# Decode attention: values two tiles behind their scores

## The chip, the cores and the metric

The kernel runs on one core of one Trainium2 chip. The metric is the time of one execution on the device, in microseconds (us), as the median of several runs. In the rows, PE is TensorE (PEld its weight loads), DVE is VectorE, ACT is ScalarE, POOL is GpSimd, and SP is the engine whose queue issues the loads.

## What is computed

One decode step of attention: 8 batches of 32 heads, one query row for each, 4096 keys and values of 128 elements, all in bf16.

```python
B, H, Sq, Skv, Dh = 8, 32, 1, 4096, 128

def reference(q, k, v):
    scale = q.shape[-1] ** -0.5
    scores = jnp.einsum('bhqd,bhkd->bhqk', q, k) * scale
    attn = _softmax(scores, axis=-1)
    return jnp.einsum('bhqk,bhkd->bhqd', attn, v)
```

Every head has its own K and V, and each element of them is used once: 256 heads x 4096 x 128 x 2 bytes = 268 MB for K and the same for V, 536.9 MB in all.

## The kernel before, in words

The 256 heads are taken four at a time: a tile is 4 heads, so there are 64 tiles (NT). A tile's K is one buffer of 128 partitions x 128 positions x 128 elements (4 MB); 32 partitions hold one head. V has the same form. K and V tiles share one pool of five buffers (SLOTS, tag `kv`), filled by `load` (line 98) from the SP queue: one DMA for a tile, but four pieces for the last V.

The work of a tile t is cut into functions, whose instructions the rows name by line and by tile:

- `product(t, lo, hi)` (line 126): VectorE multiplies K by the query row in place (line 132) and adds the two halves of each row of 128 (line 135), 32 positions at a time, so four such pairs make a tile. It is called for the first half and for the second half of the positions.
- `sum_over_d(t)` (line 142): TensorE sums the 64 remaining elements of each position down to 4, with 16 matmuls against the identity into `ps` (line 149). Each of the 16 reads all positions, so all need the whole product.
- `weights_of(t)` (line 156): VectorE reduces `ps` to the scores `sc` (line 159), takes their maximum (`pmax`, `spread`, `nmax`, lines 163 to 170) and makes `bias` (line 174); ScalarE does four exponentials, one for each head, into the weights `w` with their sums in `esum` (line 180); TensorE adds the sums over the partitions (`zp`, line 185) and VectorE takes the reciprocal `rz` (line 187).
- `values_of(t)` (line 192): TensorE multiplies weights and V in 32 matmuls into `av` (line 197), ScalarE copies the result to `comb` (line 202), four small matmuls put its diagonal blocks together in `op` (line 205), and ScalarE scales it by `rz` into `stage` (line 212). The results of eight tiles leave together (line 216).

The query rows are spread over the partitions by `q_prep` (line 112), once for four tiles.

The loop over t (lines 220 to 232) loads K of t+1 and V of t, and then does the first half of t's product, the weights of t-1, the second half of t's product, the values of t-1, and the sums of t. The program's order is a priority: the tile framework puts each engine's instructions in order by it and by when it takes them to be ready, hands out the buffers of a pool as they come free, and sets the semaphores. Each engine, and each queue of loads, then runs its own list strictly in order. So in the rows the weights of a tile (`sc` to `bias`) are woven into the second half of the next tile's product, and four of the 16 sums of t stand ahead of the values of t-1 on TensorE, the other twelve behind them.

A load needs a free buffer. K's buffer is free when the 16 sums of its tile are done, V's when the 32 matmuls of `av` are.

Of the kernel before, what the change touches and what calls it, by code (L numbers as in the profile page):

```python
# [19 lines left out]
def kernel(  # L20
# [15 lines left out]
    NT = NH // G  # L36
# [14 lines left out]
    kv_pool = ctx.enter_context(tc.tile_pool(name="kv_pool", bufs=SLOTS))  # L51
    consts = ctx.enter_context(tc.tile_pool(name="consts", bufs=1))
    q_pool = ctx.enter_context(tc.tile_pool(name="q_pool", bufs=2))
    w_pool = ctx.enter_context(tc.tile_pool(name="w_pool", bufs=2))
    small = ctx.enter_context(tc.tile_pool(name="small", bufs=3))
    o_pool = ctx.enter_context(tc.tile_pool(name="o_pool", bufs=2))
    ps_s = ctx.enter_context(tc.tile_pool(name="ps_s", bufs=2, space=bass.MemoryType.PSUM))
    ps_v = ctx.enter_context(tc.tile_pool(name="ps_v", bufs=2, space=bass.MemoryType.PSUM))
# [39 lines left out]
    def load(kind, t):  # L98
        src = k_t if kind == "k" else v_t
        buf = kv_pool.tile([P, C, D], BF16, name=f"{kind}t", tag="kv")  # L100
        cuts = [C]
        if kind == "v" and t == NT - 1:
            cuts = [C // 2, C // 4, C // 8, C // 8]
        c0 = 0
        for n in cuts:
            nc.sync.dma_start(buf[:, c0 : c0 + n, :], src[t, :, c0 : c0 + n, :])
            c0 += n
        loads[kind, t] = buf
# [3 lines left out]
    def q_prep(t):  # L112
        if t % QN == 0:
            qrow = q_pool.tile([G, QN, D], BF16, name="qrow", tag="qrow")
            nc.gpsimd.dma_start(qrow[:], q_g[:, t : t + QN, :])  # L115
            qp = ps_q.tile([P, QN * D], F32, name="qp", tag="qp")
            nc.tensor.matmul(  # L117
                qp[:], lhsT=sel[:], rhs=qrow.rearrange("g n d -> g (n d)"), start=True, stop=True
            )
            qb = q_pool.tile([P, QN, D], BF16, name="qb", tag="qb")  # L120
            nc.scalar.activation(out=qb.rearrange("p n d -> p (n d)"), in_=qp[:], func=ACT.Copy)  # L121
            qbs[t // QN] = qb

    state = {}

    def product(t, lo, hi):
        kt = loads["k", t]
        qb = qbs[t // QN]
        j = t % QN
        for c0 in range(lo, hi, MC):  # L130
            part = kt[:, c0 : c0 + MC, :]
            nc.vector.tensor_tensor(  # L132
                out=part, in0=part, in1=qb[:, j : j + 1, :].to_broadcast([P, MC, D]), op=ALU.mult
            )
            nc.vector.tensor_tensor(  # L135
                out=part[:, :, 0 : D // 2], in0=part[:, :, 0 : D // 2],
                in1=part[:, :, D // 2 : D], op=ALU.add,
            )
# [3 lines left out]
    def sum_over_d(t):  # L142
        kt = loads.pop(("k", t))
        sums[t] = []
        for u in range(NU):
            ps = ps_s.tile([P, UC, DS], F32, name="ps", tag="ps")
            n = D // 2 // DS
            for s in range(n):
                nc.tensor.matmul(  # L149
                    ps[:], lhsT=ident[:],  # L150
                    rhs=kt[:, u * UC : (u + 1) * UC, s * DS : (s + 1) * DS],
                    start=(s == 0), stop=(s == n - 1),
                )
            sums[t].append(ps)

    def weights_of(t):
        sc = small.tile([P, C], F32, name="sc", tag="sc")
        for u, ps in enumerate(sums.pop(t)):
            nc.vector.tensor_reduce(  # L159
                out=sc[:, u * UC : (u + 1) * UC], in_=ps[:], axis=AX.X, op=ALU.add  # L160
            )
        pmax = small.tile([P, 1], F32, name="pmax", tag="pmax")
        nc.vector.tensor_reduce(out=pmax[:], in_=sc[:], axis=AX.X, op=ALU.max)  # L163
        spread = small.tile([P, 32], F32, name="spread", tag="spread")
        nc.vector.tensor_scalar(  # L165
            out=spread[:], in0=zero[:], scalar1=pmax[:, 0:1], scalar2=-scale,
            op0=ALU.add, op1=ALU.mult,
        )
        nmax = small.tile([P, 1], F32, name="nmax", tag="nmax")
        nc.vector.tensor_reduce(  # L170
            out=nmax[:], in_=spread[:], axis=AX.X, op=ALU.min, apply_transpose=True
        )
        bias = small.tile([P, G], F32, name="bias", tag="bias")
        nc.vector.tensor_scalar(  # L174
            out=bias[:], in0=own[:], scalar1=nmax[:, 0:1], scalar2=None, op0=ALU.add
        )
        w = w_pool.tile([P, C, G], BF16, name="w", tag="w")
        esum = small.tile([P, G], F32, name="esum", tag="esum")
        for g in range(G):
            nc.scalar.activation(  # L180
                out=w[:, :, g], in_=sc[:], func=ACT.Exp, bias=bias[:, g : g + 1], scale=scale,
                accum_out=esum[:, g : g + 1],
            )
        zp = ps_z.tile([G, 1], F32, name="zp", tag="zp")
        nc.tensor.matmul(zp[:], lhsT=esum[:], rhs=ones[:], start=True, stop=True)  # L185
        rz = small.tile([G, 1], F32, name="rz", tag="rz")
        nc.vector.reciprocal(out=rz[:], in_=zp[:])  # L187
        state[t] = (w, rz)

    stages = {}  # L190

    def values_of(t):
        w, rz = state.pop(t)
        vt = loads.pop(("v", t))
        av = ps_v.tile([CB * G, CB * D], F32, name="av", tag="av")
        for c0 in range(0, C, CB):
            nc.tensor.matmul(  # L197
                av[:], lhsT=w[:, c0 : c0 + CB, :], rhs=vt[:, c0 : c0 + CB, :],
                start=(c0 == 0), stop=(c0 == C - CB),
            )  # L200
        comb = small.tile([CB * G, CB * D], BF16, name="comb", tag="comb")
        nc.scalar.activation(out=comb[:], in_=av[:], func=ACT.Copy)  # L202
        op = ps_o.tile([G, D], F32, name="op", tag="op")
        for m in range(CB):
            nc.tensor.matmul(  # L205
                op[:], lhsT=ident[0 : CB * G, m * G : (m + 1) * G],
                rhs=comb[:, m * D : (m + 1) * D], start=(m == 0), stop=(m == CB - 1),
            )
        if t % ON == 0:
            stages[t // ON] = o_pool.tile([G, ON, D], BF16, name="stage", tag="stage")  # L210
        stage = stages[t // ON]
        nc.scalar.activation(out=stage[:, t % ON, :], in_=op[:], func=ACT.Copy, scale=rz[:, 0:1])  # L212
        if t == NT - 1 or t == NT - 2 or (t % ON == ON - 1):
            lo = {NT - 1: NT - 1, NT - 2: NT - ON}.get(t, t - ON + 1)
            eng = nc.scalar if t == NT - 1 else nc.gpsimd
            eng.dma_start(o_g[:, lo : t + 1, :], stage[:, lo % ON : t % ON + 1, :])

    q_prep(0)
    load("k", 0)
    for t in range(NT):  # L220
        if t + 1 < NT:
            load("k", t + 1)
        load("v", t)
        if t + 2 < NT:
            q_prep(t + 2)
        product(t, 0, C // 2)
        if t > 0:
            weights_of(t - 1)
        product(t, C // 2, C)
        if t > 0:  # L230
            values_of(t - 1)
        sum_over_d(t)
    weights_of(NT - 1)
    values_of(NT - 1)


# [28 lines left out]
```

## Time and profile before

| what | value |
|---|---|
| median of 3 runs | 1394.6 us (1394.41 to 1395.68) |
| the profiled execution | 1393.52 us, of which the span from the first to the last instruction is 1391.7 us |
| bytes read | 536.94 MB, 386 GB/s over the span |
| mean granted TensorE clock | 0.807 of the full clock |

The profile is of one execution. Its rows give starts in us from the beginning of the span. In a timeline, "x4" is a run of four such instructions on one engine, with the start of the first and the time to the end of the last; in brackets stands the idle time of the engine ahead of it and who ended it. In the windows, the granted clock is a share of the full one: 1.00 is 2.4 GHz, and 0.50 is 1.2 GHz. The DMA share is the busy share of the core's 16 DMA engines; it can come out a little over 1.

### The profile page before, as it was taken

To read this page: it belongs to the slowest core of one execution; us is meant where nothing else is said; L and a number is where in the kernel's file an instruction comes from. 1 tells how busy PE (TensorE), PEld (TensorE's weight loads), DVE (VectorE), ACT (ScalarE), POOL (GpSimd) and SP (SyncE) were. 2 spreads that over 40 slices of the span, in tenths; PEclk is the share of its full clock that TensorE was granted. 3 is DMA by queue.
4 is the path that set the end of the run, shared out by engine and by line. 5 is a ranking of instruction groups with operands and counts; after the bars stand their busy time and mean duration, and the time that the engine had idled before them with its cause. 6 is when DMAs were issued, how large, how long until landed. Compare 5 with 4: busy or idle time off the path is not lost.

```text
span 1391.7 us, 9050 instructions
## 1 busy us (share of the span) xinstructions
PE 856.0 (62%) x3472; PEld 305.0 (22%) x3472; DVE 946.5 (68%) x898; ACT 182.3 (13%) x657; POOL 15.7 (1%) x36
## 2 busy tenths in 40 slices
PE   2557557566576575675665755756657557566566
PEld 0212122122122221221222212212212222122122
DVE  6766766767667667676776677676766766767662
ACT  0111111111111111111111111111111111111111
POOL 1000000000000000000000000000000000000000
PEclk9887878788787887877878878788787878788788
DMA  9999999999999899999999999999999999989970
GB/s 407 427 431 433 425 388 398 409 378 408 379 391 420 368 404 393 392 392 392 398 401 388 382 407 393 382 401 386 412 392 377 411 378 390 421 364 407 393 332 1
DMA packets 19683, 537.59 MB, mean 386 GB/s; under 512 B 2776, under 2 KB 2844, under 8 KB 3128
## 3 DMA queue, kind: packets, MB, share of 16 engines
q1 hardware_dynamic: 18864, 536.88, 92.1%
q8 instruction: 27, 0.44, 0.1%
q0 software_dynamic: 768, 0.14, 0.1%
q14 instruction: 16, 0.13, 0.0%
q10 hardware_dynamic: 8, 0.00, 0.0%
HBM read 536.94 MB, written 0.07 MB: 386 GB/s over the span
## 4 chain that ended last, share of the span: by engine, by line
PE 52%; DVE 38%; ACT 8%; issue 1%; DMA 1%; DVEq 0%; ACTq 0%
PE av L197 37%; DVE kt L132 21%; PE ps L149 13%; DVE kt L135 11%; ACT w L180 8%; DVE sc L159 3%; PE op L205 1%; DVE pmax L163 1%; DMA kt<-in_k_dram 1%; PE zp L185 1%; DVE bias L174 1%; DVE spread L165 1%; DVE nmax L170 1%; DVEq L159 0%; ACTq L180 0%
## 5 line engine op out<-in xcount | busy, mean ns | idle before, releaser
L132 DVE TENSOR_TENSOR kt<-kt,qb 128x4096 bf16<-128x4096 bf16 x256 | 577.6, 2275 | 12.4 <-DMA kt<-in_k_dram 12.4
L149 PE MATMUL ps<-kt,ident 128*128 128x512 bf16 x1024 | 308.3, 440 | 410.8 <-DVE kt L135 410.2
L197 PE MATMUL av<-vt,w 128*16 128x512 bf16 x2048 | 523.6, 420 | 0.0
L135 DVE TENSOR_TENSOR kt<-kt 128x2048 bf16<-128x2048 bf16 x256 | 305.1, 1210 | 0.0
L197 PEld LDWEIGHTS <-w 128*16 128x16 bf16 x2048 | 193.8, 97 | 299.1 <-issue 102.8
L149 PEld LDWEIGHTS <-ident 128*128 128x128 bf16 x1024 | 95.2, 103 | 666.9 <-issue 591.7
L159 DVE TENSOR_REDUCE sc<-ps 128x128 f32<-128x512 f32 x64 | 44.2, 691 | 283.8 <-PE ps L149 283.8
L180 ACT ACTIVATE w<-sc,bias 128x128 bf16<-128x128 f32 x256 | 110.8, 567 | 505.9 <-DVE bias L174 505.9
L202 ACT ACTIVATE comb<-av 16x512 bf16<-16x512 f32 x64 | 37.6, 587 | 532.9 <-PE av L197 532.9
L187 DVE RECIPROCAL rz<-zp 4x1 f32<-4x1 f32 x64 | 9.9, 155 | 135.4 <-PE zp L185 135.4
L117 PE MATMUL qp<-qrow,sel 4*128 4x512 bf16 x16 | 9.3, 582 | 110.4 <-ACT qb L121 95.6
L180 ACT ACTIVATION_READ_ACCUMULATOR w<-sc,bias 128x1 f32 x256 | 64.6, 252 | 0.0
L212 ACT ACTIVATE stage<-op,rz 4x128 bf16<-4x128 f32 x64 | 22.9, 358 | 44.2 <-PE op L205 44.2
L121 ACT ACTIVATE qb<-qp 128x512 bf16<-128x512 f32 x16 | 9.6, 597 | 122.9 <-DVE kt L132 114.0
L205 PE MATMUL op<-comb,ident 16*4 16x128 bf16 x256 | 24.3, 213 | 0.7 <-ACT comb L202 0.7
L185 PEld LDWEIGHTS zp<-ones,esum 128*4 128x4 f32 x128 | 5.8, 84 | 68.3 <-ACT w L180 68.3
L185 PE MATMUL zp<-ones,esum 128*4 128x1 f32 x128 | 12.3, 165 | 10.7 <-ACT w L180 4.2
L205 PEld LDWEIGHTS <-ident 16*4 16x4 bf16 x256 | 12.4, 78 | 27.8 <-issue 27.8
L115 POOL DMA_DIRECT2D qrow<-in_q_dram x16 | 9.3, 581 | 756.5 <-PE qp L117 756.5
L163 DVE TENSOR_REDUCE pmax<-sc 128x1 f32<-128x128 f32 x64 | 17.8, 278 | 0.0
L165 DVE TENSOR_SCALAR spread<-zero,pmax 128x32 f32<-128x32 f32 x64 | 15.0, 234 | 0.0
L174 DVE TENSOR_SCALAR bias<-own,nmax 128x4 f32<-128x4 f32 x64 | 14.3, 223 | 0.0
(18 smaller groups left out, 22.8 us busy)
## 6 DMA issues: line engine op xcount, KB each, us to landing
kt<-in_k_dram SPq DMA_DIRECT2D x64, 4096.0 KB, 19.9
vt<-in_v_dram SPq DMA_DIRECT2D x63, 4096.0 KB, 12.8
vt<-in_v_dram SPq DMA_DIRECT2D x1, 2048.0 KB, 14.3
vt<-in_v_dram SPq DMA_DIRECT2D x1, 1024.0 KB, 16.4
vt<-in_v_dram SPq DMA_DIRECT2D x2, 512.0 KB, 17.6
qrow<-in_q_dram POOLq DMA_DIRECT2D x16, 4.0 KB, 6.8
out_dram<-stage POOLq DMA_DIRECT2D x7, 8.0 KB, 6.7
out_dram<-stage POOLq DMA_DIRECT2D x1, 7.0 KB, 1.9
```

Of the source, the lines that this page charges most:

```text
L132: nc.vector.tensor_tensor(out=part, in0=part, in1=qb[:, j : j + 1, :].to_broadcast([P, MC, D]), op=ALU.mult)
L135: nc.vector.tensor_tensor(out=part[:, :, 0 : D // 2], in0=part[:, :, 0 : D // 2], in1=part[:, :, D // 2 : D], op=ALU.add,)
L149: nc.tensor.matmul(ps[:], lhsT=ident[:], rhs=kt[:, u * UC : (u + 1) * UC, s * DS : (s + 1) * DS], start=(s == 0), stop=(s == n - 1),)
L159: nc.vector.tensor_reduce(out=sc[:, u * UC : (u + 1) * UC], in_=ps[:], axis=AX.X, op=ALU.add)
L163: nc.vector.tensor_reduce(out=pmax[:], in_=sc[:], axis=AX.X, op=ALU.max)
L165: nc.vector.tensor_scalar(out=spread[:], in0=zero[:], scalar1=pmax[:, 0:1], scalar2=-scale, op0=ALU.add, op1=ALU.mult,)
L174: nc.vector.tensor_scalar(out=bias[:], in0=own[:], scalar1=nmax[:, 0:1], scalar2=None, op0=ALU.add)
L180: nc.scalar.activation(out=w[:, :, g], in_=sc[:], func=ACT.Exp, bias=bias[:, g : g + 1], scale=scale, accum_out=esum[:, g : g + 1],)
L185: nc.tensor.matmul(zp[:], lhsT=esum[:], rhs=ones[:], start=True, stop=True)
L197: nc.tensor.matmul(av[:], lhsT=w[:, c0 : c0 + CB, :], rhs=vt[:, c0 : c0 + CB, :], start=(c0 == 0), stop=(c0 == C - CB),)
L202: nc.scalar.activation(out=comb[:], in_=av[:], func=ACT.Copy)
L205: nc.tensor.matmul(op[:], lhsT=ident[0 : CB * G, m * G : (m + 1) * G], rhs=comb[:, m * D : (m + 1) * D], start=(m == 0), stop=(m == CB - 1),)
```

## The change

The values of a tile are taken two tiles after its scores. The loop does the values of t-2 where it did those of t-1, and the last two tiles' values stand behind the loop. The sum of the weights and its reciprocal (`zp`, `rz`) move from `weights_of` to the head of `values_of`. V's loads move back by one place: K0 and K1 are loaded ahead of the loop, and turn t loads K of t+2 and then V of t. The weights get three buffers for two, and the small tiles four for three. The five buffers of K and V stay.

```diff
-    w_pool = ctx.enter_context(tc.tile_pool(name="w_pool", bufs=2))
-    small = ctx.enter_context(tc.tile_pool(name="small", bufs=3))
+    w_pool = ctx.enter_context(tc.tile_pool(name="w_pool", bufs=3))
+    small = ctx.enter_context(tc.tile_pool(name="small", bufs=4))
...
                 accum_out=esum[:, g : g + 1],
             )
+        state[t] = (w, esum)
+
+    stages = {}
+
+    def values_of(t):
+        w, esum = state.pop(t)
         zp = ps_z.tile([G, 1], F32, name="zp", tag="zp")
         nc.tensor.matmul(zp[:], lhsT=esum[:], rhs=ones[:], start=True, stop=True)
         rz = small.tile([G, 1], F32, name="rz", tag="rz")
         nc.vector.reciprocal(out=rz[:], in_=zp[:])
-        state[t] = (w, rz)
-
-    stages = {}
-
-    def values_of(t):
-        w, rz = state.pop(t)
         vt = loads.pop(("v", t))
...
     load("k", 0)
+    load("k", 1)
     for t in range(NT):
-        if t + 1 < NT:
-            load("k", t + 1)
+        if t + 2 < NT:
+            load("k", t + 2)
         load("v", t)
...
         product(t, C // 2, C)
-        if t > 0:
-            values_of(t - 1)
+        if t > 1:
+            values_of(t - 2)
         sum_over_d(t)
     weights_of(NT - 1)
+    values_of(NT - 2)
     values_of(NT - 1)
```

## Rows read from the trace of the kernel before

**Rows 1.** The page: busy time of the engines, and transfers in 40 slices

```profile
PE 856.0 (62%) x3472; PEld 305.0 (22%) x3472; DVE 946.5 (68%) x898; ACT 182.3 (13%) x657; POOL 15.7 (1%) x36
...
DMA  9999999999999899999999999999999999989970
GB/s 407 427 431 433 425 388 398 409 378 408 379 391 420 368 404 393 392 392 392 398 401 388 382 407 393 382 401 386 412 392 377 411 378 390 421 364 407 393 332 1
```

**Rows 2.** Waits of the engines: who waited for whom, us in total, times, longest

```profile
DVE sc L159 <- PE ps L149: 283.8, 63, 10.5
DVE rz L187 <- PE zp L185: 135.4, 64, 2.4
...
DVE kt L132 <- DMA kt<-in_k_dram: 12.4, 1, 12.4
```

**Rows 3.** Waits of the load queue (SP), same columns

```profile
SPq L106 <- PE av L197: 1085.3, 61, 18.8
```

**Rows 4.** Timeline of one tile: start us, us, engine, line, operation, [idle before]

```profile
607.08 0.69 DVE L159 TENSOR_REDUCE sc<-ps 128x128 f32<-128x512 f32 x1 [3.82 <-PE ps L149]
...
614.82 0.22 DVE L174 TENSOR_SCALAR bias<-own,nmax 128x4 f32<-128x4 f32 x1
614.96 1.87 PE L149 MATMUL ps<-kt,ident 128*128 128x512 bf16 x4 [7.98 <-DVE kt L135]
...
616.98 9.16 PE L197 MATMUL av<-vt,w 128*16 128x512 bf16 x32
...
617.24 4.46 DVE L132 TENSOR_TENSOR kt<-kt,qb 128x4096 bf16<-128x4096 bf16 x2
617.36 0.13 PEld L197 LDWEIGHTS <-w 128*16 128x16 bf16 x1 [0.29 <-issue]
...
620.77 0.13 PEld L197 LDWEIGHTS <-w 128*16 128x16 bf16 x1 [0.29 <-issue]
...
621.63 2.34 DVE L135 TENSOR_TENSOR kt<-kt 128x2048 bf16<-128x2048 bf16 x2
...
626.08 1.04 PE L149 MATMUL ps<-kt,ident 128*128 128x512 bf16 x4
...
629.37 0.69 DVE L159 TENSOR_REDUCE sc<-ps 128x128 f32<-128x512 f32 x1 [5.39 <-PE ps L149]
```

**Rows 5.** Timeline, load queue (SP): the first V that waited, and the last

```profile
50.90 0.33 SPq L106 DMA_DIRECT2D vt<-in_v_dram  x1
...
1330.25 4.96 SPq L106 DMA_DIRECT2D vt<-in_v_dram  x5
```

**Rows 6.** Windows: us, busy of PE, PEld, DVE, ACT, POOL, granted clock, DMA share, GB/s

```profile
52.00:100.00 48.00, 27.67 (x120) 10.05 (x118) 34.41 (x34) 6.31 (x22) 0.57 (x1) 0.85 1.00 431
100.00:148.00 48.00, 28.76 (x112) 10.10 (x111) 32.72 (x32) 6.51 (x26) 0.00 (x0) 0.75 1.00 431
...
400.00:800.00 400.00, 254.50 (x1031) 90.49 (x1031) 275.60 (x261) 53.87 (x195) 4.04 (x7) 0.80 0.94 393
```

**Rows 7.** Windows over one `av`, same columns

```profile
616.98:621.20 4.22, 4.22 (x12) 1.28 (x13) 4.04 (x3) 0.00 (x0) 0.00 (x0) 0.50 0.88 380
621.20:626.07 4.87, 4.87 (x23) 1.92 (x21) 2.77 (x3) 0.00 (x0) 0.00 (x0) 0.99 0.75 320
```

**Rows 8.** Timeline, the first product

```profile
13.39 4.49 DVE L132 TENSOR_TENSOR kt<-kt,qb 128x4096 bf16<-128x4096 bf16 x2 [12.41 <-DMA kt<-in_k_dram]
```

**Rows 9.** Timeline of the tail

```profile
1364.27 7.59 PE L197 MATMUL av<-vt,w 128*16 128x512 bf16 x32
...
1375.08 0.69 DVE L159 TENSOR_REDUCE sc<-ps 128x128 f32<-128x512 f32 x1 [10.48 <-PE ps L149]
...
1376.65 0.23 DVE L174 TENSOR_SCALAR bias<-own,nmax 128x4 f32<-128x4 f32 x1
...
1378.81 8.75 PE L197 MATMUL av<-vt,w 128*16 128x512 bf16 x32
...
1387.60 0.59 ACT L202 ACTIVATE comb<-av 16x512 bf16<-16x512 f32 x1 [8.90 <-PE av L197]
```

## The prediction

> **What bounds the kernel now.** I read the page first, to see which resource has no slack in any slice. It shows no simple answer [rows 1]: TensorE is busy for 62% of the span, VectorE for 68%, the transfers look nearly full in every slice, and yet the rate falls from 427 to 433 GB/s in slices 2 to 4 to about 390 later. So I asked the waits who is late. VectorE waited for a K tile once in the whole run, at the very start, for 12.4 us [rows 2]; no compute instruction waits for V at all. It waited 283.8 us for the sums of the products (`ps`), and 135.4 us for the sum of the weights (`zp`). The load queue, on the other side, stood 1085.3 us waiting for the values' matmuls (`av`) to give a buffer back [rows 3]. The data are early, the buffers are late: a loop of compute sets the pace, and the transfers follow it.
>
> The loop is read from one tile in the timeline [rows 4]. From `sc` at 607.08 to the end of `bias` at 615.04 VectorE needs 7.96 us (it does the second half of the next tile's product in between). Then ScalarE's four exponentials, until `av` starts at 616.98: 1.94 us. Then the 32 matmuls of `av`, until the sums go on at 626.08: 9.10 us. Then the remaining 12 sums and the four `op` matmuls, until the next `sc` at 629.37: 3.29 us. Together 22.29 us, and every link waits for the one before. This tile is one of the long ones: from V_2's issue at 50.90 to V_62's at 1330.25 [rows 5] it is 1279.35 / 60 = 21.32 us a tile.
>
> What the transfers could do is seen where they had not yet been held up: 431 GB/s at a share of 1.00 between 52 and 148 us, against 393 at 0.94 later [rows 6]. Each load is 4.194 MB, so one takes 4.194 / 0.431 = 9.73 us and a tile (K and V) 19.46 us. That is 1.86 us under the loop.
>
> **The change, part by part.** *The lag.* `av` of tile t-2 takes weights that were finished a tile ago. So it leaves the loop: after the sums of t-1, TensorE can run `av` of t-2 while VectorE works on tile t, and the sums of t follow the product of t. VectorE's own work for a tile is 7.96 us for `sc` to `bias` with the second half, and 623.97 - 617.24 = 6.73 us for the first half [rows 4]: 14.7 us. TensorE's, at the full clock: 12 sums and 4 `op` in 3.2 us and 4 sums at about 0.24, so some 3.8 us for 16 sums; and `av` in 9.1 us as it is here, which holds a stretch at half the clock (0.50 from 616.98 to 621.20, then 0.99) [rows 7]. That makes 13.4 us with `op`. Both are under 19.46, and they overlap but for sums and `sc`. So the loop gives way and the transfers bind.
>
> *Do the buffers then let the transfers run without a gap?* Loads go out as K0, K1, K2, V0, K3 at once; each further one needs a release. Releases come as sums 0, sums 1, values 0, sums 2, values 1, ..., so V1 follows sums 0, K4 sums 1, V2 values 0, K5 sums 2: V_t follows values t-2, and K_(t+3) follows sums t. Let K_t land at X. VectorE ends its product at X + 14.7; V_(t-2) lands at X + 9.7; values t-2 run to about X + 18.8, sums t to X + 23. V_t is issued at X + 18.8 and the stream comes to it at X + 38.9; K_(t+3) at X + 23, and the stream comes to it at X + 48.6. Each has 20 us in hand. VectorE needs sums t for `sc` only after the first half of t+1, at X + 26.2. So every wait of a tile is hidden under the stream; where this cover is thinnest (3 us, before `sc`), losing it delays VectorE, which has 19.46 - 14.7 = 4.8 us of slack a tile.
>
> *K ahead of V.* The queue issues the same 131 loads. V_0 lands one place (9.7 us) later; its use moves a whole tile later. Cost nil.
>
> *`zp` and the reciprocal.* Same instructions, 0.15 us on VectorE. The 2.1 us wait of each [rows 2] was for exponentials that are now a tile old: it goes, off the path that binds, so I count nothing; were `zp` queued behind a late `av`, the wait would come out of the 4.8 us. *The extra buffers* (3 and 4) only keep the longer-lived tiles; nothing.
>
> *The end.* The first K landed at 13.39 [rows 8]. The last load is number 127 after it: 13.39 + 127 x 9.73 = 1249.1; V_61 is 1229.6, V_62 1239.4. From there: values 61 to 1238.1 (8.5 us, half of it at the lower clock), sums 63 to 1241.9, `sc` to `av` takes 3.7 us in today's tail, so the last weights are ready by 1245.6 beside values 62 (7.6 us in the tail [rows 9], to 1249.5), and values 63 to 1257.1. From the end of the last `av` to the end of the span 4.1 us pass today (1387.6 to 1391.7, with `comb`, `op`, stage and store): 1261.2. The added values of tile 62 cost 7.6 us of this, as they now stand behind the last sums. The profiled execution took 1393.5 us for a span of 1391.7, and the median of the runs is 1.1 us above it: 1261.2 + 1.8 + 1.1 = **1264 us**, 9.4% below 1394.6. A gain of 130 us is 62 tiles by 1.86 = 115, and the rest from the tail: today 61 us of compute follow the issue of the last V [rows 5].
>
> **The rivals.** *1. The stream does not hold 431.* The later windows move 393 at 0.94, which is 418 at a full share [rows 6]; I take the gaps for late issues, but they could be the price of busier engines on the same memory, and VectorE is to be busier still. At 418 a load takes 10.03 us, the last lands at 1287, and the time is 1302. Chance 0.13. At its harshest the stream could give no more than the run's mean of 386 [rows 1]: 536.9 / 0.386 = 1391 us for the loads, no gain; 96 us at 431 speak against it: 0.01. The Trainium skill (DMA: Bandwidth & Descriptors, Bandwidth) says that loads from HBM are bound by some 358 GB/s for a core; an estimate from that page's figure is 1500 us for these loads alone. The trace speaks against it: this very kernel averaged 386 GB/s. The same section gives 425 GB/s measured for a lone 16 MB load, an estimate of 1263 us for the loads and so some 1278 in all, between my two cases.
>
> *2. `sc` in front of the first half (slower than before).* The order of each engine is the scheduler's, and a scheduler that believes the K tile late may put `sc` to `bias` of t ahead of the whole product of t+1. Then VectorE stands still during the sums, and the loop is product (2 x 6.73 = 13.5), 16 sums, and `sc` to `bias` alone (1375.08 to 1376.88 in the tail, 1.8 [rows 9]). With sums at 3.8 us this is 19.1, still under the stream; with TensorE at the lower clock, where a matmul takes 0.426 us (its weight loads go from 617.36 to 620.77 in 8 steps [rows 4], at 0.50 [rows 7]), the sums take 6.8 and the loop 22.1 us: 62 x 0.78 = 48 us more, **1443 us**. It decides from sums of 6.0 us on (21.32 - 15.3). For it: TensorE would idle before the sums, and idle stretches are followed by half the clock today. Against: today's order has the first half in front all through. Chance 0.06.
>
> *3. TensorE at the lower clock throughout.* 48 matmuls at 0.426 and 0.6 us of others are 21.0 us a tile: 62 x 1.54 = 95 more than forecast, 1359. It needs the clock never to rise in a stretch of 13 us; today it does after 4 to 6. Chance 0.05.
>
> *4. The edit does not move `av`.* TensorE's queue today runs 4 sums before `av` [rows 4]. If it keeps that order, those 4 take the time of the exponentials and the loop stays: 7.96 + 1.9 + 9.1 + 3.3, no change, 1395. They came first, though, since the weights were not there, which now they are. Chance 0.03.
>
> **How the numbers follow.** Forecast 0.72, rival 1 0.13 (and 0.01 without a gain), 2 0.06, 3 0.05, 4 0.03. Faster by over 0.2% (2.8 us, about what a measurement of this kernel can tell from no change): 0.72 + 0.13 + 0.05 = 0.90; within it 0.04; slower 0.06. The range takes forecast and rival 1: down to 1252 (433 GB/s as in the best slice takes 5 us off, an `av` of the last tile that runs beside its pieces' landing another 7), up to 1312 (rival 1 and 10 us for a tail at the lower clock). It leaves out 0.15.
>
> **What would show it.** Right: VectorE's largest wait becomes a K transfer, some 4 us a tile; TensorE waits for V at `av`; GB/s is near 431 in all slices but the last; the load queue still waits, but each load is issued some 20 us before its first packet; `av` starts before the product of the same turn ends. Wrong: 415 to 420 GB/s at a full share (1); `sc` directly behind `ps` with VectorE idle in between (2); a granted clock near 0.5 (3); `av` still behind 4 sums (4).

## The result and the profile after

The changed kernel takes 1269.5 us (median of 4 runs, 1268.67 to 1270.69) against 1394.6 us (4 runs): a ratio of 0.910, 95% interval 0.909 to 0.912. Forecast were 1264 us in a range of 1252 to 1312. The profiled execution took 1270.69 us for a span of 1268.9 us.

The page of the changed kernel: busy times, transfers in 40 slices, and the shares of the chain that ended last.

```profile
PE 847.7 (67%) x3472; PEld 315.7 (25%) x3472; DVE 939.4 (74%) x898; ACT 181.7 (14%) x657; POOL 15.8 (1%) x36
...
DMA  9999999999999999999999999999999999999994
GB/s 397 433 431 432 432 431 429 431 432 429 430 430 429 431 433 431 430 430 431 430 430 433 430 431 431 429 431 430 433 429 430 433 430 433 430 429 430 430 432 178
...
DMA 69%; PE 25%; DVE 5%; ACT 0%; issue 0%; ACTq 0%; DVEq 0%
```

No engine became quicker: the busy times are those of before to within 11 us [rows 1]. What changed is the row of GB/s. It stands at 429 to 433 in every slice between the first and the last, where before it fell to about 390 [rows 1, 6], and the chain that sets the end runs through transfers for 69% of the span.

The waits of the changed kernel (who waited for whom: us in total, times, longest):

```profile
PE av L197 <- DMA vt<-in_v_dram: 349.0, 57, 7.9
DVE kt L132 <- DMA kt<-in_k_dram: 283.5, 57, 12.3
...
DVE sc L159 <- PE ps L149: 28.2, 5, 11.5
```

Against [rows 2] the direction has turned round. VectorE's wait for the sums fell from 283.8 to 28.2 us, and its wait for a K tile rose from 12.4 us (once) to 283.5 us (57 times, 5 us each). TensorE waits for V, which nobody did before. The load queue still waits:

```profile
SPq L106 <- PE av L197: 572.2, 61, 21.4
```

These 572.2 us are put down to `av` (1085.3 before [rows 3]), and another 560 us to V's transfers and to `zp`. But its waits now cost nothing: the median time from issue to landing is 29.8 us for a V and 35.5 us for a K (12.8 and 19.9 before), which less one transfer of 9.7 us leaves some 20 and 26 us in hand.

One tile in the timeline of the changed kernel (start, us, engine, line, operation, [idle before]), to be laid beside [rows 4]:

```profile
600.51 4.50 DVE L132 TENSOR_TENSOR kt<-kt,qb 128x4096 bf16<-128x4096 bf16 x2 [4.72 <-DMA kt<-in_k_dram]
...
607.20 0.68 DVE L159 TENSOR_REDUCE sc<-ps 128x128 f32<-128x512 f32 x1
...
610.25 8.99 PE L197 MATMUL av<-vt,w 128*16 128x512 bf16 x32 [6.85 <-DMA vt<-in_v_dram]
...
614.97 0.21 DVE L174 TENSOR_SCALAR bias<-own,nmax 128x4 f32<-128x4 f32 x1
...
619.17 1.04 PE L149 MATMUL ps<-kt,ident 128*128 128x512 bf16 x4
...
619.93 4.49 DVE L132 TENSOR_TENSOR kt<-kt,qb 128x4096 bf16<-128x4096 bf16 x2 [4.76 <-DMA kt<-in_k_dram]
```

The row to read first is `av`: it starts at 610.25, ahead of `bias` at 614.97, so its weights are a turn old; before, it stood 2 us behind `bias` [rows 4]. A tile takes 619.93 - 600.51 = 19.42 us, twice a load, and both engines stand idle for a transfer once in it (4.7 and 6.9 us).

### The profile page after: what moved, and what is told of

The parts are those of the page before. It is cut to its first block, busy times and chain, and to the rows that moved or that the text cites. A ratio compares the mean times of both kernels' runs of the same rounds, so it can differ in the third digit from the quotient of the medians.

```text
span 1268.9 us, 9053 instructions
## 1 busy us (share of the span) xinstructions
PE 847.7 (67%) x3472; PEld 315.7 (25%) x3472; DVE 939.4 (74%) x898; ACT 181.7 (14%) x657; POOL 15.8 (1%) x36
## 4 chain that ended last, share of the span: by engine, by line
DMA 69%; PE 25%; DVE 5%; ACT 0%; issue 0%; ACTq 0%; DVEq 0%
DMA vt<-in_v_dram 68%; PE av L197 24%; DVE kt L132 3%; DVE kt L135 1%; PE ps L149 1%; DMA kt<-in_k_dram 1%; ACT w L180 0%; DVE sc L159 0%; PE op L205 0%; ACT comb L202 0%; DVE pmax L163 0%; DVE spread L165 0%; DVE bias L174 0%; ACT qb L121 0%; PE qp L117 0%
## 5 line engine op out<-in xcount | busy, mean ns | idle before, releaser
L197 PE MATMUL av<-vt,w 128*16 128x512 bf16 x2048 | 573.8, 450 | 349.0 <-DMA vt<-in_v_dram 349.0
L132 DVE TENSOR_TENSOR kt<-kt,qb 128x4096 bf16<-128x4096 bf16 x256 | 579.4, 2285 | 283.5 <-DMA kt<-in_k_dram 283.5
L197 PEld LDWEIGHTS <-w 128*16 128x16 bf16 x2048 | 208.8, 102 | 696.4 <-issue 529.8
L149 PE MATMUL ps<-kt,ident 128*128 128x512 bf16 x1024 | 248.7, 385 | 24.0 <-DVE kt L135 24.0
L149 PEld LDWEIGHTS <-ident 128*128 128x128 bf16 x1024 | 89.6, 97 | 156.4 <-issue 58.9
L159 DVE TENSOR_REDUCE sc<-ps 128x128 f32<-128x512 f32 x64 | 43.8, 684 | 28.2 <-PE ps L149 28.2
L205 PEld LDWEIGHTS <-ident 16*4 16x4 bf16 x256 | 12.8, 78 | 33.0 <-issue 33.0
L174 DVE TENSOR_SCALAR bias<-own,nmax 128x4 f32<-128x4 f32 x64 | 13.6, 212 | 0.0
L170 DVE TRANSPOSE_TENSOR_REDUCE nmax<-spread 128x1 f32<-128x32 f32 x64 | 13.1, 205 | 0.1
## 6 DMA issues: line engine op xcount, KB each, us to landing
kt<-in_k_dram SPq DMA_DIRECT2D x64, 4096.0 KB, 35.5
vt<-in_v_dram SPq DMA_DIRECT2D x63, 4096.0 KB, 29.8
```

Of the source, the lines that this page charges most:

```text
L132: nc.vector.tensor_tensor(out=part, in0=part, in1=qb[:, j : j + 1, :].to_broadcast([P, MC, D]), op=ALU.mult)
L149: nc.tensor.matmul(ps[:], lhsT=ident[:], rhs=kt[:, u * UC : (u + 1) * UC, s * DS : (s + 1) * DS], start=(s == 0), stop=(s == n - 1),)
L159: nc.vector.tensor_reduce(out=sc[:, u * UC : (u + 1) * UC], in_=ps[:], axis=AX.X, op=ALU.add)
L197: nc.tensor.matmul(av[:], lhsT=w[:, c0 : c0 + CB, :], rhs=vt[:, c0 : c0 + CB, :], start=(c0 == 0), stop=(c0 == C - CB),)
L205: nc.tensor.matmul(op[:], lhsT=ident[0 : CB * G, m * G : (m + 1) * G], rhs=comb[:, m * D : (m + 1) * D], start=(m == 0), stop=(m == CB - 1),)
```

## The experiments

Three questions: which part of the change does it, what the loads' place is worth, and how far the changed kernel is from the limit that it now has.

**Loads alone.** The kernel before, with V's loads moved back and nothing else:

```diff
     load("k", 0)
+    load("k", 1)
     for t in range(NT):
-        if t + 1 < NT:
-            load("k", t + 1)
+        if t + 2 < NT:
+            load("k", t + 2)
```

> The kernel before, with only the loads moved (K two tiles ahead, V one place back). Theory: the loop stays, so no gain. The instruction lists differ from before, though: zp now stands behind av on TensorE and the reciprocal still ahead of the first half on VectorE, so the loop is 7.96 + 1.94 + av 8.2 + 0.4 + first half 6.73 = 25.2 us for 21.3: about 1635 us (1560 to 1700). Rival (the deeper prefetch of K is what brings the gain): about 1270 us.

Measured: 1274.7 us, ratio 0.914 (0.913 to 0.916). The theory, with its 1635 us, fell, and the rival's 1270 us is close (its number, but not its reason: `e11` below has the same loads and gains nothing). This part alone gives 120 of the 125 us. Its timeline shows why:

```profile
609.96 9.51 PE L197 MATMUL av<-vt,w 128*16 128x512 bf16 x32 [6.72 <-DMA vt<-in_v_dram]
...
614.64 0.22 DVE L174 TENSOR_SCALAR bias<-own,nmax 128x4 f32<-128x4 f32 x1
...
619.30 0.19 PE L185 MATMUL zp<-ones,esum 128*4 128x1 f32 x2
619.42 0.82 PE L149 MATMUL ps<-kt,ident 128*128 128x512 bf16 x3
...
619.54 0.15 DVE L187 RECIPROCAL rz<-zp 4x1 f32<-4x1 f32 x1 [4.68 <-PE zp L185]
```

Here too `av` starts ahead of `bias`. The source still says "values of t-1", but with V later in the loads' order the framework wrote TensorE's list differently: all 16 sums of t (and `op`) ahead of `av` of t-1, where four stood ahead of it before [rows 4]. One thing stayed as it was, the sum of the weights: `zp` now stands behind an `av`, and VectorE waits for it in nearly every tile. The waits of this run:

```profile
PE av L197 <- DMA vt<-in_v_dram: 343.2, 56, 8.1
DVE rz L187 <- PE zp L185: 248.1, 61, 5.4
```

These 248 us cost next to nothing (4.1 us a tile, out of the 4.8 that the stream leaves VectorE). What this run lacks against the changed kernel stands in its tail:

```profile
1255.04 0.39 PE L149 MATMUL ps<-kt,ident 128*128 128x512 bf16 x1
...
1255.47 0.69 DVE L159 TENSOR_REDUCE sc<-ps 128x128 f32<-128x512 f32 x1 [10.92 <-PE ps L149]
...
1259.20 8.75 PE L197 MATMUL av<-vt,w 128*16 128x512 bf16 x32
```

The last of the 16 sums of tile 63 stands behind `av` of tile 62. So the last `sc`, and the exponentials, come after that `av`, and the last `av` ends at 1267.95; in the changed kernel it ends at 1264.70 (in the chain further below). The spans of the two profiled executions differ by just as much, 3.3 us (the medians by 5.2).

**The lag alone.** The changed kernel with the loads of before:

```diff
     load("k", 0)
-    load("k", 1)
     for t in range(NT):
-        if t + 2 < NT:
-            load("k", t + 2)
+        if t + 1 < NT:
+            load("k", t + 1)
```

> The changed kernel, with the loads as before (K one tile ahead, V in its old place). By buffers alone the stream would have 15 us in hand and the time would be about 1274 us (a tail 5 us longer, since the last K lands one place later). But VectorE's list now has sc to bias ahead of the whole product, which is my second rival: the loop is product 13.5 + 16 sums + 1.8. With sums that start at half the clock after some 6 us of idle time (5.5 us) it is 20.8 us a tile: 1345 us (1290 to 1410). At 1270 the order of the list does no harm; at 1395 the loads' move was the whole gain.

Measured: 1426.1 us, ratio 1.023 (1.021 to 1.024): slower than the kernel before, and above the range expected. Its timeline:

```profile
619.38 0.69 DVE L159 TENSOR_REDUCE sc<-ps 128x128 f32<-128x512 f32 x1 [5.40 <-PE ps L149]
...
620.95 0.23 DVE L174 TENSOR_SCALAR bias<-own,nmax 128x4 f32<-128x4 f32 x1
...
625.99 0.15 DVE L193 RECIPROCAL rz<-zp 4x1 f32<-4x1 f32 x1 [4.82 <-PE zp L191]
626.08 4.49 DVE L132 TENSOR_TENSOR kt<-kt,qb 128x4096 bf16<-128x4096 bf16 x2
...
639.57 6.22 PE L149 MATMUL ps<-kt,ident 128*128 128x512 bf16 x16 [12.29 <-DVE kt L135]
...
645.82 0.69 DVE L159 TENSOR_REDUCE sc<-ps 128x128 f32<-128x512 f32 x1 [6.31 <-PE ps L149]
```

This is the order that the prediction's rival 2 feared. VectorE's list has `sc` to `bias` of t-1 ahead of the whole product of t. So VectorE idles through the sums (6.31 us, with TensorE at a granted clock of 0.57 after 12.29 us of idleness), and the loop is `sc` to `bias`, product, sums, one after another. By itself this is not slower than before: in the steady state three turns in four take 20.6 to 21.0 us from `sc` to `sc`, where the mean before was 21.3. What makes it slower is the fourth turn, the one shown. There `rz` stands ahead of the product as well and waits for a `zp` that is queued behind 30 matmuls of `av`: 26.4 us from `sc` to `sc`. Thirteen such turns bring the mean to 21.8 us. VectorE's waits for `zp`:

```profile
DVE rz L193 <- PE zp L191: 67.6, 14, 5.0
```

**The sum of the weights left where it was.** The changed kernel with `zp` and `rz` back in `weights_of`:

```diff
             )
-        state[t] = (w, esum)
-
-    stages = {}
-
-    def values_of(t):
-        w, esum = state.pop(t)
         zp = ps_z.tile([G, 1], F32, name="zp", tag="zp")
...
         nc.vector.reciprocal(out=rz[:], in_=zp[:])
+        state[t] = (w, rz)
+
+    stages = {}
+
+    def values_of(t):
+        w, rz = state.pop(t)
```

> The changed kernel, with zp and the reciprocal back in weights_of. On TensorE zp of t-1 now stands behind 8 of the 32 matmuls of av of t-2, and waits there for the exponentials. Theory: the 2 to 4 us of it are covered by the stream; 1271 us (1268 to 1276). Rival (zp's move is what brings the gain): 1395 us.

Measured: 1377.3 us, ratio 0.988 (0.986 to 0.989): all but 17 us of the gain is gone. Its waits, and the tile in its timeline:

```profile
PE zp L185 <- ACT w L180: 494.5, 63, 10.2
```

```profile
620.16 1.89 PE L197 MATMUL av<-vt,w 128*16 128x512 bf16 x8
...
628.01 0.22 DVE L174 TENSOR_SCALAR bias<-own,nmax 128x4 f32<-128x4 f32 x1
...
630.39 0.19 PE L185 MATMUL zp<-ones,esum 128*4 128x1 f32 x2 [8.34 <-ACT w L180]
630.45 8.14 PE L197 MATMUL av<-vt,w 128*16 128x512 bf16 x24
```

`zp` of t-1 stands in TensorE's list behind eight matmuls of `av` of t-2. It needs the exponentials of the turn, so TensorE stops there, for 8.3 us in this tile and 7.8 us in the mean, with the 24 other matmuls of `av`, which could run, and the sums queued behind one small one. The exponentials are back in the loop.

**Is VectorE's wait for `zp` a cost?** The kernel before, without the reciprocal and the scaling by it:

```diff
-        rz = small.tile([G, 1], F32, name="rz", tag="rz")
-        nc.vector.reciprocal(out=rz[:], in_=zp[:])
...
-        nc.scalar.activation(out=stage[:, t % ON, :], in_=op[:], func=ACT.Copy, scale=rz[:, 0:1])
+        nc.scalar.activation(out=stage[:, t % ON, :], in_=op[:], func=ACT.Copy)
```

> The kernel before, with the reciprocal left out (the output stays unnormalised), so that VectorE's 135.4 us of waits for zp are gone. Theory (the loop sc, exponentials, av, sums sets the pace): VectorE stands 2.1 us longer at its next wait for the sums instead; 1394.6 us, within 4. Rival (the gain came from moving zp and the reciprocal out of VectorE's way): 2.1 us x 63 less, about 1262 us.

Measured: 1395.8 us, ratio 1.000 (0.999 to 1.001). The 135.4 us of [rows 2] were free: VectorE's wait for the sums grew from 283.8 to 427.2 us in their place.

```profile
DVE sc L159 <- PE ps L149: 427.2, 63, 12.7
```

**Lists against loads.** In these runs the loads' place changed the lists as well. Two runs tried to hold a few instructions: `e9`, the new loads with the fifth sum of t held behind `av` of t-1 and `sc` behind the first half, and `e10`, the changed kernel with the old loads, `sc` behind the first half and `zp` behind the sums.

> The loads of the changed kernel, but values at lag 1, with TensorE's list held as before (4 sums of t, zp and av of t-1, 12 sums of t) and sc of t-1 behind the first half of t. In the run with the loads alone the values had slipped behind the sums, a lag of two tiles made by the list. Theory (what counts is that av, and the exponentials it waits for, stand between the product and the sums on TensorE's list): the loop of 21.3 us is back, 1395 us (1375 to 1415). Rival (where the loads stand is what counts, by the buffers): 1275 us.

> The values at lag 2 with the loads as before, and the lists held as in the changed kernel (sc of t-1 behind the first half of t, zp of t-2 behind the sums of t-1). Theory (the list): the stream binds again, with 15 us in hand for each load; about 1276 us (1270 to 1290), a few us over the changed kernel since the last K lands one place later. Rival (the loads' place): between 1395 and the 1426 that lag 2 with these loads gave.

Measured: 1338.7 us (ratio 0.957, 0.953 to 0.962) and 1338.1 us (0.959, 0.958 to 0.960), both between the two answers, and both inconclusive. The framework reordered what was not held. In `e9` `sc` to `bias` stood alone in every other tile (606.62 to 608.41). In `e10` `rz` stood ahead of the product and waited 363.9 us for `zp`, 63 times.

So for the next two every instruction of TensorE and VectorE was held to the order of the text, and the text was written out in the order of one list or the other. `e11` has the new loads and the lists of the kernel before; `e12` differs from it by this:

```diff
-    load("k", 1)
     for t in range(NT):
-        if t + 2 < NT:
-            load("k", t + 2)
+        if t + 1 < NT:
+            load("k", t + 1)
...
+        if t > 1:
+            zsum(t - 2)
+            late = lambda: recip(t - 2)
...
+        if t > 1:
+            values_of(t - 2)
         sum_over_d(t, 0, 4)
-        if t > 0:
-            zsum(t - 1)
-            recip(t - 1)
-            values_of(t - 1)
-        sum_over_d(t, 4, 8)
-        if t > 0:
-            out_of(t - 1)
-        sum_over_d(t, 8, 16)
+        if t > 1:
+            out_of(t - 2)
+        sum_over_d(t, 4, 16)
```

> The loads and buffers of the changed kernel, with every instruction of TensorE and VectorE held in the order that the kernel before has. Theory (the order of the lists decides): the loop of 21.3 us, 1395 us (1385 to 1405). Rival (the loads' place decides): 1270 to 1275 us. A time between the two would mean that both count.

> The loads of the kernel before, with every instruction of TensorE and VectorE held in the order that the changed kernel has (the reciprocal too, which in the run before this stood ahead of the first half and waited there for the sums). Theory (the lists): the stream binds, 1275 us (1270 to 1285). Rival (the loads' place): 1340 us or more.

| | lists of before | lists of the changed kernel |
|---|---|---|
| loads of before | 1394.6 us | 1278.0 us (`e12`; 0.917, 0.915 to 0.918) |
| loads moved | 1394.0 us (`e11`; 1.000, 0.999 to 1.001) | 1269.6 us (changed kernel, second run of it) |

Both as expected. In the last cell alone the lists were not held; held lists and moved loads stand together only in the run with the shorter tail below, at 1271.6 us. `e11` also has the extra buffers for the weights and the small tiles, so these alone bring nothing. The waits of `e11` are those of before [rows 2] within a microsecond, although its V loads are moved:

```profile
DVE sc L162 <- PE ps L152: 283.0, 63, 10.7
```

Those of `e12` are of the new kind, although its loads are the old ones:

```profile
DVE kt L132 <- DMA kt<-in_k_dram: 312.7, 63, 12.5
```

The lists of the two engines decide 117 of the 125 us. By itself the loads' place is worth nothing under the old lists and 8.4 us under the new ones. These are at the end: with the old order the last K lands behind V of tile 61, and the last product waits for it. It starts at 1236.07 in `e12`, and at 1226.50 in the changed kernel:

```profile
1236.07 4.49 DVE L132 TENSOR_TENSOR kt<-kt,qb 128x4096 bf16<-128x4096 bf16 x2 [4.83 <-DMA kt<-in_k_dram]
```

```profile
1226.50 4.49 DVE L132 TENSOR_TENSOR kt<-kt,qb 128x4096 bf16<-128x4096 bf16 x2 [4.78 <-DMA kt<-in_k_dram]
```

**How far is the limit?** The loads of the changed kernel through the same five buffers, with the attention replaced by one small VectorE copy for each K and V tile:

```diff
-            nc.vector.tensor_tensor(
-                out=part, in0=part, in1=qb[:, j : j + 1, :].to_broadcast([P, MC, D]), op=ALU.mult
-            )
...
+        sc = small.tile([P, D], BF16, name="sc", tag="sc")
+        nc.vector.tensor_copy(out=sc[:], in_=kt[:, C - 1, :])
...
+        nc.vector.tensor_copy(out=stage[:, t % ON, :], in_=vt[0:G, C - 1, :])
```

> The loads of the changed kernel through the same five buffers, with the compute left out: one small copy reads each tile and frees it (the output is not the attention). Theory (the stream's own rate bounds the changed kernel): 128 loads at 9.73 to 9.78 us and a short end, 1258 us (1252 to 1264), the same 430 GB/s. Rival (busy engines slow the stream): faster loads than beside the compute, under 1248 us.

Measured: 1255.9 us, ratio 0.900 (0.899 to 0.902). The window from 400 to 800 us of this run, and of the changed kernel:

```profile
400.00:800.00 400.00, 0.00 (x0) 0.00 (x0) 7.74 (x41) 0.00 (x0) 1.17 (x2) 1.00 1.00 431
```

```profile
400.00:800.00 400.00, 276.65 (x1127) 102.62 (x1126) 297.27 (x282) 58.68 (x213) 4.05 (x7) 0.84 1.00 431
```

The busy engines take no bandwidth that the window could show. The changed kernel is 13.6 us above its loads (14.6 between the two profiled executions). Most of this is work behind the last transfer: the last piece of V lands at 1251.4 in the loads alone, 2.9 us ahead of the end, and at 1255.7 in the changed kernel, 13.2 us ahead of it. The other 4.3 us are made in the stream.

**Buffers.** The changed kernel with four K and V buffers:

```diff
-SLOTS = 5
+SLOTS = 4
```

> The changed kernel with four buffers for K and V instead of five; its lists are the same. Theory (each load is issued some 20 us before the stream comes to it): one buffer less takes one load's 9.7 us of that, 10 us are left, no change: 1270 us (1268 to 1275). Rival (the depth of the loads is what the gain hangs on): 1300 us or more.

Measured: 1279.8 us, ratio 0.918 (0.916 to 0.919), some 10 us above five buffers and 5 above the range expected. The steady windows are full with four as well (430 GB/s from 400 to 800 us), so the loss is made once, at the start:

```profile
64.00:128.00 64.00, 38.63 (x163) 14.59 (x164) 48.21 (x41) 8.47 (x31) 0.57 (x1) 0.81 0.87 365
```

With five, the same 64 us run at 428 GB/s.

**A shorter tail.** The changed kernel's lists, held, with V of tile 61 ahead of the last K and that K in four pieces (V of 62 in two, of 63 in three), beside the changed kernel once more:

```diff
+        if kind == "k" and t == NT - 1:
+            cuts = [MC] * (C // MC)
+        if kind == "v" and t == NT - 2:
+            cuts = [C // 2, C // 2]
...
+        if t == NT - 3:
+            load("v", t)
```

> The changed kernel with its own lists held, and another end: the V of the third tile from the end is loaded ahead of the last K, the last K comes in four pieces, the V before the last in two, the last V in three. From the traced tail: values 61 can start at 1230, ahead of the last sums, which end at 1244; values 62 to 1251, values 63 to 1258.5, end of the span at 1262.7: about 1264 us, 5 us under the changed kernel. If the tail hangs on the last V's landing alone, no gain.

> The changed kernel once more, on the same chip as the run with the short tail, to compare the two: 1269.5 us, within 2.

Measured: 1271.6 us (0.912, 0.910 to 0.913) and 1269.6 us (0.910, 0.909 to 0.912): no gain. The tail in the timeline of the first:

```profile
1229.20 7.07 PE L217 MATMUL av<-vt,w 128*16 128x512 bf16 x32
...
1243.52 1.86 PE L156 MATMUL ps<-kt,ident 128*128 128x512 bf16 x4 [7.25 <-DVE kt L142]
...
1245.83 3.45 PE L156 MATMUL ps<-kt,ident 128*128 128x512 bf16 x12
...
1249.26 7.07 PE L217 MATMUL av<-vt,w 128*16 128x512 bf16 x32
...
1257.37 7.07 PE L217 MATMUL av<-vt,w 128*16 128x512 bf16 x32
```

`av` of tile 61 was done 10 us earlier, as meant (1236.3 against 1246.2). But the last product then ended only at 1243.4, TensorE idled for 7.25 us before the sums and began them at half clock (0.50 over the first four, 0.80 over the other twelve), and the two `av` begin within 1.1 us of where they begin in the changed kernel (1250.35 and 1257.31, in the chain further below).

## Why the prediction was right, and where it was not

**What binds before, and after: right.** A loop through `sc`, `bias`, the exponentials, `av` and the sums set the pace [rows 4], and without it the stream does, at 431 GB/s and a share of 1.00. Rival 1 is refuted by the windows and by the loads alone; rival 3 by a granted clock of 0.84; rival 4 by `av` ahead of `bias`. Each of the signs named came: VectorE's wait for K (5 us a tile, some 4 forecast), TensorE's for V, 429 to 433 GB/s, loads issued some 20 us ahead of their transfer, and `av` started before the product of its turn ended.

**"It leaves the loop", because of the lag: incomplete.** The forecast took TensorE's order from the new source. What takes `av` out of the loop is its place in TensorE's list, and the source sets this only together with the loads: the lag with the old loads is slower than before, the loads without the lag give nearly all of the gain, and with the lists held the loads' place does not matter to the loop. The number was right because the change, as a whole, got the lists that the forecast assumed. That the moved loads brought them was luck: the forecast counted the move as nil, and without it the same source takes 1426.1 us.

**"K ahead of V ... Cost nil": failed.** As a transfer it does cost nothing in the loop (`e11`). But it is the part that turns the lists, and at the end it brings the last K one place forward, worth 8.4 us (`e12`).

**"`zp` ... off the path that binds, so I count nothing": right for VectorE, silent on TensorE.** VectorE's waits for it are free twice over (135.4 us before, 248.1 us with the loads alone). But the step priced only VectorE's side. On TensorE a `zp` that needs the current exponentials stops the `av` queued behind it: 494.5 us of waits, and 1377.3 us in place of 1269.5.

**Rival 2, 0.06: did not happen, but its order is real, and its price was near by luck.** The order came with the lag and the old loads. Rival 2 had sums at half clock throughout, 6.8 us and 22.1 us a tile, and so 1443 us. In that run VectorE waits 5.7 us in the mean for the sums (356.0 us in 63 waits) and most turns take 20.6 to 21.0 us. An estimate from these turns, without the 5.7 us more of each of the thirteen long ones, is some 1350 us, faster than before. The rest of the 1426 us comes with the turns in which VectorE waits for `zp` ahead of the product (4.8 us each), which rival 2 did not have.

**The sum: 5.5 us short.** The terms that were mis-sized stand in the chain that ended last in the changed kernel:

```profile
1206.37 29.81 DMA vt<-in_v_dram
...
1236.23 10.02 PE av L197 x32
...
1250.35 6.93 PE av L197 x32
...
1257.31 0.67 PE av L197 x3
...
1258.33 6.37 PE av L197 x29
```

The stream is the larger: V of tile 61 landed at 1236.2, forecast was 1229.6, so 6.6 us. A load took (1226.50 - 13.28) / 124 = 9.78 us up to the last K, not 9.73. From there to the end of the span it is 32.7 us for 31.6: `av` of tile 61 took 10.0 us, not 8.5, with a granted clock of 0.50 over its first 4.8 us (TensorE had idled for 5.8 us before it), and the shorter terms behind it gave 0.4 us back. The last term went the other way: the profiled execution was 1.2 us above the median, where I had put the median 1.1 us above it, 2.3 us less. 6.6 + 1.1 - 2.3 = 5.4.

The 0.05 us a load are not spread evenly. VectorE takes up the K tiles 19.42 to 19.5 us apart nearly throughout, but 20.2 to 20.5 us apart at 405, 562, 718, 875, 1031 and 1188 us. In this trace that is one step of some 1 us every eight tiles, 57 to 59 us behind each store of eight tiles' results. But in the trace of the second run of the same kernel such steps come at 211, 582, 875, 953 and 1188 us, out of that order, so the stores are not shown to make them. The loads alone store as often, and from 150 us on none of their steps is over 0.4 us. What takes the time when the engines are busy stays open.

**What was not tried:** a list for the tail in which the last product, the sums and both `av` are interleaved by hand. The 13.6 us over the loads alone are the most that any order could still give with these transfers; some 10 of them lie behind the last transfer.

## What to carry to other kernels

Where a framework orders the engines' lists, take the order from the trace (which instruction stands ahead of which on each engine), not from the source: moving a load can change it as much as moving the work, and a matmul that waits for another engine stops everything that is queued behind it, however small it is. To tell a list's effect from a load's, hold every instruction of the engines in question; holding a few let the others move and settled nothing. And once a stream binds, an engine's wait costs nothing until it exceeds what the stream leaves that engine (here 4.8 us a tile), so what is left is the work behind the last transfer.

## What the runs showed of the hardware

**After idle time, `av` begins at the lower clock.** The windows of the changed kernel over the wait before an `av`, its first part and its rest (busy of PE, PEld, DVE, ACT, POOL, granted clock, DMA share, GB/s):

```profile
603.00:610.20 7.20, 0.40 (x4) 0.12 (x3) 7.20 (x7) 0.00 (x0) 0.00 (x0) 0.80 0.97 419
610.25:614.40 4.15, 4.15 (x11) 1.39 (x11) 4.15 (x7) 0.60 (x1) 0.00 (x0) 0.53 0.97 418
614.40:619.20 4.80, 4.80 (x24) 1.85 (x23) 0.78 (x2) 1.73 (x8) 0.00 (x0) 1.00 1.00 427
```

After 6.9 us of waiting for V, the first 4.15 us of `av` run at 0.53 and the rest at 1.00, so the 32 matmuls take 9.0 to 10.0 us; where TensorE came straight from other matmuls they took 7.07 us (the tail with the shorter pieces, above). In the loop the 2 to 3 us are covered by the stream. In the tail they are on the chain.

**One core's load stream.** 537 MB came through one queue of 4 MB loads at 431 GB/s, with the engines idle or two thirds busy. The Trainium skill (DMA: Bandwidth & Descriptors, Bandwidth) names some 358 GB/s for a core where both cores that share the memory stream, 425 GB/s measured for a lone 16 MB load with the neighbour idle, and 435 GB/s as the ceiling of the ports. These runs, with one core at work, agree with the last two: 1.4% above the measured figure and 1% under the ceiling, held for 1.2 ms. The first, from which the prediction's 1500 us were worked out, is for two cores that stream; no run here shows that case.
